# Last group's second channel product: three of seven outer products with tokens stationary, and a shared sum joined once

## The chip, the cores and the metric

The kernel runs on one core of one Trainium2 chip. The metric is the device time of one execution in microseconds (us). The time before is the median of three runs, 780.99 us (780.35 to 781.89). One more execution was taken by the hardware profiler. All times below that carry a place ("at 762.0") are us from the start of that execution's span.

TensorE (PE) multiplies matrices and writes PSUM; PEld is its weight load. VectorE (DVE), ScalarE (ACT) and GpSimd (POOL) do the rest. SyncE (SP), ScalarE and GpSimd issue DMAs.

## The reference

Inputs are q, k, v of shape (8 batches, 8 heads, 576, 64), a norm weight and four mixer weights. The part that matters here is the end:

```python
x = attention(q, k, v, g_norm)                 # (8, 576, 512)
h = np.maximum(x.T @ w_tok1, 0.0) @ w_tok2     # token mixing
u = x + h.T
h2 = np.maximum(u @ w_ch1, 0.0) @ w_ch2        # w_ch1 512 x 1536, w_ch2 1536 x 512
return u + h2
```

The change concerns the last product, `max(...) @ w_ch2`, and the addition to `u`, for the last two batches. All is float32.

## The kernel before, in words

The attention and the token mixing come first and put `u` into the output tensor in DRAM, 512 rows of each batch, and the remaining 64 rows of all batches into a ninth unit `u_rest`. Then the channel part runs over nine units of 512 rows. Unit 0 is done alone. The others go in pairs, as groups 1 to 4; the last group (g = 4) holds units 6 and 7.

In a group, both channel products are done by Strassen's scheme in Winograd's form, at two levels. The outer level has seven products (numbered 1 to 7), and each of these has seven inner products with the same numbers. The outer results of the second channel product are four quarters (i, j) of the group's output: i is the unit of the pair (unit 6 or unit 7), and j is the half of the 512 columns. With r1 to r7 for the outer results, quarter (0, 0) is r1 + r2, quarter (0, 1) is r1 + r6 + r5 + r3, quarter (1, 0) is r1 + r6 + r7 + r4, and quarter (1, 1) is r1 + r6 + r7 + r5. The sum r1 + r6 is shared by three of them. Each quarter is also added to `u`.

`outer` (line 871) writes down one outer product. It puts seven inner products at places in a list `products`, and the steps of the other engines in `beside`. Lines 1423 to 1427 then play the list place by place. So the order of all instructions on every engine is written out by hand: `put(b + place, ...)` says at which place a step is issued, where b is seven times the number of the outer product that begins the channel product. `PLACE` and `LAST` say at which place each inner product stands; the inner product 4 of an outer product stands after the first two of the next one. The last group takes its outer products in the order 1, 4, 7, 6, 5, 3, 2, the others in the order 1, 2, 4, 7, 6, 5, 3.

The PSUM banks are "a" and "b" (one each) and "d" (two). Inner product 1 fills "a"; ScalarE copies it into "d", where 6, 7 and 4 are added. Inner product 5 fills "b", and 3 is added there. Before bank "d" and bank "b" are written again, `read` saves their present state as `u2` and `p5`. Each inner result is a quarter of an outer result (128 x 256 elements) and is copied or added into it.

There are two ways to multiply (`mul`, lines 1038 to 1049). In the usual one the weights are stationary: 3 matmuls of 128 x 256 per inner product (six instructions in the profile), and the result has output columns on partitions and tokens along the free side. It lies transposed to the output, in blocks of 32. `turn` (line 1182) transposes such a tile by 32 x 32 blocks on VectorE. `put_rows` (line 1197) turns a tile and adds it to the output in DRAM by four DMAs on GpSimd that accumulate, each 128 KB in pieces of 256 B (64 columns). In the other way the tokens are stationary: 6 matmuls of 128 x 128 per inner product (twelve instructions), and the result has tokens on partitions. It lies by rows as the output does, with 256 columns in 1 KB. Before the change only outer product 2 of the last group does so (`END`).

In the last group (lines 1169 to 1174) r1 is copied to `xs`, turned and added to unit 6's left half by four accumulating DMAs. Later `fetch_last` reads that half back by rows into `xs`, product 2 is added onto it, and `store_last` writes it by four plain stores of 128 KB. Unit 6's right half is kept in a tile `xg`. It was fetched by `fetch_x` (line 599) and turned during the group before. Onto it go r1 + r6 (`xadd(6)`), r5 (`xadd(5)`) and, quarter by quarter, product 3. `store_part` (line 1202) turns it in two halves and stores it in eight pieces of 64 KB. Unit 7's two halves are joined by `join`, which is `put_rows`: r4 + r7 + r6 + r1 into the left and r7 + r6 + r1 + r5 into the right.

Of the kernel before, what the change touches and what calls it, by code (L numbers as in the profile page):

```python
# [11 lines left out]
F32 = mybir.dt.float32  # L12
# [3 lines left out]
ALU = mybir.AluOpType  # L16
# [4 lines left out]
def kernel(  # L21
# [32 lines left out]
    nc = tc.nc  # L54
    P = 128
    B, S, DM = k.shape
# [4 lines left out]
    J, JJ, HF = 4, 5, 64  # L61
    LO = P * J
    assert D == 64 and DM == 512 and S == LO + HF and B % 2 == 0
    NC, NF, NTOK = DM // P, DCH // P, DTOK // P
    HP = H // 2
    DH = DM // 2
# [5 lines left out]
    NG = 1 + B // 2  # L72
    T = 2 * P
# [4 lines left out]
    def pool(name, bufs, side="left", stack=ctx, **kw):  # L78
        return stack.enter_context(tc.tile_pool(name=name, bufs=bufs, side=side,
                                                reuse_waits="tile", **kw))  # L80
# [4 lines left out]
    left, right = ExitStack(), ExitStack()  # L85
# [24 lines left out]
    u_rows = lambda u: u_rest if u == B else out[u, :LO]  # L110

    def do(f, *a, **kw):
        return lambda: f(*a, **kw)

    late = {}


    keep = tc.keep_in_program_order

    def dma(o, i, engine=nc.sync):  # L120
        keep(engine.dma_start(o, i))

    def tensor_add(o, a, b, op=ALU.add, engine=nc.vector):
        keep(engine.tensor_tensor(out=o, in0=a, in1=b, op=op))  # L124
# [4 lines left out]
    def copy(o, a):  # L129
        keep(nc.scalar.copy(o, a))  # L130

    def matmul(*a, **kw):
        keep(nc.tensor.matmul(*a, **kw))  # L133
# [458 lines left out]
    xg, xt, uT = {}, {}, {}  # L592
    Q = 32
    NQ = T // Q

    def units(g):
        return ((0,), (1, 2), (3, 4), (5, B), (6, 7))[g] if g < NG else (NU, NU)

    def fetch_x(g):

        if g == 0:
            xg[g] = late["xg0"].tile([P, J, DM], F32, name="xg")
            dma(xg[g], u_rows(0).rearrange("(t p) e -> p t e", p=P))
        else:
            xg[g] = late["xg"].tile([P, 2 * NQ, 2, Q], F32, name="xg")
            for b in range(NC):
                dma(xg[g][ds(b * Q, Q)].rearrange("p n l j -> p n (l j)"),
                    u_rows(units(g)[0])[:, ds(DH + b * HF, HF)].rearrange("(n i) e -> i n e", i=Q))

    def fetch_t(u, i):  # L610

# [251 lines left out]
    PLACE = {1: 0, 5: 1, 6: 3, 2: 4, 3: 5, 7: 6, 4: 9}  # L863
    LAST = {1: 0, 5: 1, 6: 3, 2: 4, 7: 5, 3: 6, 4: 7}
    products, beside = {}, defaultdict(list)
    END = NG - 1, 2

    def put(place, *steps):
        beside[place] += steps
# [77 lines left out]
    def halves(f):  # L947
        return [do(f, i) for i in range(2)]
# [13 lines left out]
    def w_part(n, p):  # L962
        return ws[n, POS[p] // 2][:, POS[p] % 2]

    def fetch_ahead(n):
        for k, place in enumerate((-12, -9, -7, -4)):
            if 7 * n + place >= 0:
                put(7 * n + place, do(fetch_w, n, k))
# [61 lines left out]
    def channel2(g, n0):  # L1030
        b = 7 * n0
        t = {n: do(v_tile, g, i) for n, i in FROM.items()}

        def second(i, o):
            n = n0 + i
            r = {}

            def mul(p, ps, start, stop):
                v = v_in_parts[g, o](p)
                w = w_part(n, p).rearrange("p (w e) -> p w e", w=W)  # L1040
                if (g, o) == END:
                    for t in range(2):
                        for s in range(W):
                            matmul(ps[:, ts(t, P)], lhsT=v[:, s, ts(t, P)], rhs=w[:, s],
                                   start=(start and t == 0 and s == 0), stop=stop, skip_group_check=True)
                else:
                    for s in range(W):
                        matmul(ps, lhsT=w[:, s], rhs=v[:, s], start=(start and s == 0), stop=stop,
                               skip_group_check=True)

            def to(i, j):
                if not r:
                    name = "us" if o in (1, 2, 6, 3) else "r"
                    r[0] = late[name].tile([P, 2 * NQ, 2, Q], F32, name=name, tag=name)
                return r[0][:, ts(i, NQ), j]

            if (g, o) == END:
                outer(7 * n, T, mul, lambda i, j: rows_of(xs[0])[:, ts(i, 2), j], onto=True, last=True,
                      fit=lambda flat: flat.rearrange("p (t b e) -> p t b e", t=2, b=NC))
            elif g == NG - 1 and o == 3:  # L1060
                outer(7 * n, T, mul, lambda i, j: xg[g][:, ts(i, NQ), j], onto=True)
            else:
                outer(7 * n, T, mul, to)
            fetch_ahead(n)
            return r

        rs = {}
        for i, o in enumerate(order2(g)):
            rs[o] = second(i, o)
# [47 lines left out]
            tensor_add(half(a21(), i), half(a21(), i), half(v_tile(g, 5), i))  # L1117

        radd = lambda o, a: do(lambda: tensor_add(rs[o][0], rs[o][0], rs[a][0]))
        xadd = lambda o: do(lambda: tensor_add(*2 * [xg[g]], rs[o][0]))  # L1120
        A, S1, S2, S3, S4 = (halves(f) for f in (make_a21, sum1, sum2, sum3, sum4))


# [22 lines left out]
        def join(i, j, o):  # L1146
            return do(put_rows, units(g)[i], j, lambda: rs[o][0])

        def both(o, a, c):
# [3 lines left out]

            return step

        def first_aside():
            xs[0] = late["xs"].tile([P, 2 * NQ, 2, Q], F32, name="xs")
            copy(xs[0], rs[1][0])

        if g < NG - 1:  # L1160
            for place, *steps in ((19, radd(2, 1)), (20, join(0, 0, 2)), (38, radd(6, 1)), (39, radd(7, 6)), (40, radd(4, 7)),
                                  (41, join(1, 0, 4)), (46, radd(7, 5)), (47, radd(5, 6)), (48, join(1, 1, 7)),
                                  (52, radd(3, 5)), (55, join(0, 1, 3))):
                put(b + place, *steps)
            if g == NG - 2:
                put(b + 60, do(fetch_x, g + 1))
                put(b + 79, do(turn, lambda: xg[g + 1]))
        else:
            for place, *steps in ((11, first_aside), (17, do(put_rows, units(g)[0], 0, lambda: xs[0])), (31, radd(6, 1)),
                                  (32, radd(7, 6)), (34, fetch_last), (34, radd(4, 7)), (35, join(1, 0, 4)), (36, xadd(6)),  # L1170
                                  (38, radd(7, 5)), (39, join(1, 1, 7)), (41, xadd(5)),
                                  (44, store_part(0)), (46, store_part(1)),
                                  (48, store_last(0)), (49, store_last(1))):
                put(b + place, *steps)

# [6 lines left out]
    def turn(t):  # L1182

        t = t()
        keep(nc.vector.transpose(t, t))
# [13 lines left out]
        for b, at, to in pieces(u, j):  # L1199
            keep(nc.gpsimd.dma_start(to, t()[ds(b * Q, Q), at].rearrange("p n l j -> p n (l j)"), accum_op=ALU.add))  # L1200

    def store_part(i):

        def step():
            t = xg[NG - 1][:, ts(i, NQ)]
            turn(lambda: t)
            for b in range(NC):
                dma(out[units(NG - 1)[0], ts(i, T), ds(DH + b * HF, HF)].rearrange("(n i) e -> i n e", i=Q),
                    t[ds(b * Q, Q)].rearrange("p n l j -> p n (l j)"), nc.scalar if i and b % 2 else nc.sync)

        return step

    last_rows = lambda t=0, n=J: out[units(NG - 1)[0], ds(t * P, n * P), :DH].rearrange("(t p) e -> p t e", p=P)
    rows_of = lambda x: x.rearrange("p t (b l e) -> p t l b e", b=NC, l=2)
    xs = {}

    def fetch_last():
        xs[0] = late["xs"].tile([P, J, DH], F32, name="xs")
        dma(xs[0], last_rows())

    def store_last(i):

        def step():
            for t, queue in zip((2 * i, 2 * i + 1), (nc.sync, nc.scalar)):
                dma(last_rows(t, 1), xs[0][:, ts(t, 1)], queue)

        return step

# [126 lines left out]
    for i in range(2):  # L1355
# [4 lines left out]
    last = [  # L1360
        "h00 -i3 -d31 -s30 2 -d40 2 o0", "h01 2 o1", "h10 2 o3", "h11 2 o2", "hr z2 1 o4", "u0 z3 1 c0", "u1 z4 1 c1 o5", "u2 z5 c2",
        "u3 z6 1 c3 o6", "u4 z7 1", "u5 z8 1", "u6 1 s0", "u7 s1 s2", "u8 s3 s4"]
# [15 lines left out]
    late["c"] = pool("c", 2, "left", banks, space=bass.MemoryType.PSUM)  # L1378

    fetch_x(0)  # L1380
    firsts, lasts = mix_ch2()
    parts2 = [f for o in ORDER2 for f in split(2, o)]
# [27 lines left out]
    def turn_over():  # L1410
        w2s.close()
        late["vr"] = pool("vr", 1, "right")
        late["sv"] = pool("sv", 2, "right")
        late["s3"] = pool("s3", 1, "right")
        late["xg"] = pool("xg", 1, "right")
        late["xs"] = pool("xs", 1, "right")
        late["r"] = pool("r", 3, "right")

    put(9, turn_over)
    for g in range(1, NG):  # L1420
        channel1(g, 14 * (g - 1))
        channel2(g, 14 * (g - 1) + 7)
# [40 lines left out]
```

## Time and profile before

| what | value |
|---|---|
| median of three runs | 780.99 us (780.35 to 781.89) |
| profiled execution, its own time | 777.2 us |
| its span, first to last instruction | 775.4 us, 12776 instructions |
| granted TensorE clock | 0.999 |
| PE busy | 761.0 us, 98% |
| PEld busy | 611.6 us, 79% |
| DVE busy | 643.2 us, 83% |
| ACT busy | 277.4 us, 36% |
| POOL busy | 112.4 us, 14% |
| DMA moved | 188.30 MB, mean 243 GB/s |

The busy shares are means over the whole span. The change touches the last 30 us and two steps of some 90 us before the end. So the lines that matter are those of the end: the chain of waits from the last instruction back, the instructions in order of time, and the landings of the last DMAs. In a line of the chain stand start, length and what held it; L124 is the helper for VectorE's additions, L130 ScalarE's copy, L133 the matmul, L121 the plain DMA, L1185 the turn, and L1200 the accumulating DMA.

### The profile page before, as it was taken

How to read it: one execution, taken by the hardware profiler on the slowest of the kernel's cores; microseconds unless marked ns; L12 is line 12 of the kernel's file. 1: busy time of each engine (PE TensorE's matmuls, PEld its weight loads, DVE VectorE, ACT ScalarE, POOL GpSimd, SP SyncE). 2: the span in 40 equal slices, each digit the busy share in tenths (PEclk: the TensorE clock that was granted, in tenths of full speed). 3: DMA queues.
4: the chain of work that ended last, by engine and by line, in shares of the span. 5: the costliest groups of instructions: out<-in, count | busy, mean ns of one | idle time of the engine just before them, and what ended most of it. 6: DMA issues, size and time to landing. Idle time of an engine off the chain costs nothing.

```text
span 775.4 us, 12776 instructions
## 1 busy us (share of the span) xinstructions
PE 761.0 (98%) x4682; PEld 611.6 (79%) x4682; DVE 643.2 (83%) x946; ACT 277.4 (36%) x549; POOL 112.4 (14%) x128
## 2 busy tenths in 40 slices
PE   5999999999999999999999999999999999999997
PEld 5655555545888888888888888888888888888887
DVE  2867887897776868989978889987998996798996
ACT  2566575665210233521134242223352223325220
POOL 1002021113410000002240001042000218000204
PEclk9999999999999999999999999999999999999999
DMA  9999999999899696599998577999659879855679
GB/s 293 322 330 375 370 354 281 253 259 362 281 279 358 256 301 189 166 274 184 233 230 262 148 216 224 256 188 268 199 147 285 174 218 207 207 147 159 150 192 117
DMA packets 177820, 188.30 MB, mean 243 GB/s; under 512 B 74464, under 2 KB 140512, under 8 KB 177760
## 3 DMA queue, kind: packets, MB, share of 16 engines
q1 hardware_dynamic: 140752, 167.55, 71.5%
q0 software_dynamic: 34816, 18.36, 16.1%
q10 hardware_dynamic: 2192, 1.61, 0.7%
q8 instruction: 37, 0.61, 0.3%
q14 instruction: 23, 0.19, 0.1%
HBM read 138.31 MB, written 49.15 MB: 242 GB/s over the span
## 4 chain that ended last, share of the span: by engine, by line
PE 94%; DVE 3%; DMA 1%; ACT 1%; issue 1%; SPq 0%; DVEq 0%; ACTq 0%
PE ps_d L133 27%; PE ps_b L133 19%; PE ps_a L133 18%; PE ps_u L133 8%; PE ps_h L133 8%; PE ps_v L133 5%; PE ps_c L133 3%; PE ps_o L133 2%; PE ps_kv L133 2%; PE ps_w L133 2%; DMA raw<-in_moe_w_tok_dram 1%; ACT x L499 1%; DVE r L124 0%; DVE sv L124 0%; DVE x L445 0%
## 5 line engine op out<-in xcount | busy, mean ns | idle before, releaser
L133 PE MATMUL ps_d<-ui,w 128*128 128x256 f32 x504 | 118.6, 379 | 0.0
L133 PEld LDWEIGHTS ps_d<-ui,w 128*128 128x128 f32 x504 | 95.8, 190 | 13.0
L130 ACT COPY ps_d<-ps_a 128x768 f32<-128x768 f32 (+1 forms) x56 | 32.0, 572 | 202.1 <-PE ps_a L133 199.1
L124 DVE TENSOR_TENSOR v<-v,v 128x1536 f32<-128x1536 f32 (+2 forms) x70 | 103.2, 1482 | 0.3
L133 PE MATMUL ps_b<-sv,w 128*128 128x256 f32 x324 | 79.2, 380 | 0.1
L133 PE MATMUL ps_a<-v,w 128*128 128x256 f32 x324 | 78.8, 379 | 0.0
L1200 POOL DMA_DIRECT2D out_dram<-us x24 | 26.8, 1831 | 292.6 <-ACT p L130 287.3
L133 PEld LDWEIGHTS ps_b<-sv,w 128*128 128x128 f32 x324 | 60.8, 190 | 10.2 <-issue 2.1
L133 PEld LDWEIGHTS ps_a<-v,w 128*128 128x128 f32 x324 | 61.6, 190 | 8.4
L133 PE MATMUL ps_h<-x,w_tok 128*128 128x512 f32 (+1 forms) x160 | 65.4, 603 | 0.5 <-DVE x L503 0.4
L133 PE MATMUL ps_u<-h,w_tok 128*128 128x512 f32 (+1 forms) x160 | 64.7, 599 | 0.0
L133 PE MATMUL ps_d<-v,w 128*128 128x256 f32 x258 | 62.7, 379 | 0.0
L127 ACT ACTIVATE v<-v 128x768 f32<-128x768 f32 (+1 forms) x54 | 42.6, 821 | 55.1 <-DVE v L124 55.1
L1200 POOL DMA_DIRECT2D out_dram<-r x40 | 41.3, 1923 | 103.2 <-ACT p L130 80.3
L133 PE MATMUL ps_d<-sv,w 128*128 128x256 f32 x228 | 55.4, 379 | 0.0
L133 PEld LDWEIGHTS ps_d<-v,w 128*128 128x128 f32 x258 | 48.9, 190 | 6.6
L133 PEld LDWEIGHTS ps_h<-x,w_tok 128*128 128x128 f32 (+1 forms) x160 | 26.2, 189 | 32.3 <-issue 27.3
L133 PEld LDWEIGHTS ps_u<-h,w_tok 128*128 128x128 f32 (+1 forms) x160 | 25.6, 179 | 31.1 <-issue 26.7
L133 PEld LDWEIGHTS ps_d<-sv,w 128*128 128x128 f32 x228 | 43.3, 190 | 5.9
L133 PE MATMUL ps_a<-uT,w 128*128 128x256 f32 x192 | 46.7, 379 | 0.0
L133 PE MATMUL ps_b<-ui,w 128*128 128x256 f32 x168 | 40.8, 379 | 0.0
L133 PEld LDWEIGHTS ps_a<-uT,w 128*128 128x128 f32 x192 | 36.5, 190 | 5.0
(162 smaller groups left out, 1278.0 us busy)
## 6 DMA issues: line engine op xcount, KB each, us to landing
w<-parts SPq DMA_DIRECT2D x168, 384.0 KB, 3.7
w<-parts SPq DMA_DIRECT2D x56, 192.0 KB, 3.8
uT<-blocks SPq DMA_DIRECT2D x36, 256.0 KB, 5.3
k_in<-in_k_dram SPq DMA_DIRECT2D x16, 512.0 KB, 8.7
qT<-in_q_dram SPq DMA_DIRECT2D x8, 1024.0 KB, 9.5
out_dram<-x POOLq DMA_DIRECT2D x16, 512.0 KB, 6.4
v_in<-in_v_dram SPq DMA_DIRECT2D x14, 512.0 KB, 9.0
raw<-in_moe_w_ch_dram SPq DMA_DIRECT2D x8, 768.0 KB, 7.7
```

The costliest lines, as they stand in the source:

```text
L124: keep(engine.tensor_tensor(out=o, in0=a, in1=b, op=op))
L127: keep(nc.scalar.activation(o, a, AF.Relu))
L130: keep(nc.scalar.copy(o, a))
L133: keep(nc.tensor.matmul(*a, **kw))
L499: keep(nc.scalar.activation(x[:, k, h], x[:, k, h], AF.Copy, scale=inv[:, k, h]))
L1200: keep(nc.gpsimd.dma_start(to, t()[ds(b * Q, Q), at].rearrange("p n l j -> p n (l j)"), accum_op=ALU.add))
```

## The change

Outer products 5, 3 and 2 of the last group are now all computed with tokens stationary (`ROWS` in place of `END`). Their results lie by rows. The tile `xg` of the last group, its pool, its fetch and its early turn are gone, and so are `xadd` and `store_part`.

The shared sum r1 + r6 is joined into unit 6's right half by itself, with a turn and four accumulating DMAs. Unit 7's right half gets r7 + r6 + r1 without r5, in the same way and three places earlier. r5 is added to unit 7's right half by `join_rows`: one accumulating DMA on GpSimd of 512 rows, 1 KB each. Product 3 is written into a tile of its own. The base of its quarters is r5, so the tile holds r3 + r5. It is added to unit 6's right half by two more such DMAs of 256 rows each. Product 2 is added onto `xs` and stored as before; only the form of the tile `xs` is another.

```diff
-    END = NG - 1, 2
+    ROWS = {(NG - 1, o) for o in (5, 3, 2)}
...
-                if (g, o) == END:
+                if (g, o) in ROWS:
...
-                return r[0][:, ts(i, NQ), j]
-
-            if (g, o) == END:
-                outer(7 * n, T, mul, lambda i, j: rows_of(xs[0])[:, ts(i, 2), j], onto=True, last=True,
+                return quarter(r[0], i, j) if (g, o) in ROWS else r[0][:, ts(i, NQ), j]
+
+            if (g, o) in ROWS:
+                outer(7 * n, T, mul, (lambda i, j: quarter(xs[0], i, j)) if o == 2 else to,
+                      o == 3 and (lambda i, j: quarter(rs[5][0], i, j)), onto=o == 2, last=o == 2,
                       fit=lambda flat: flat.rearrange("p (t b e) -> p t b e", t=2, b=NC))
-            elif g == NG - 1 and o == 3:
-                outer(7 * n, T, mul, lambda i, j: xg[g][:, ts(i, NQ), j], onto=True)
...
+        def join_rows(i, o, t, n):
+            keep(nc.gpsimd.dma_start(out[units(g)[i], ds(t * P, n * P), DH:].rearrange("(t p) e -> p t e", p=P),
+                                     flat(rs[o][0])[:, ds(t, n)], accum_op=ALU.add))
...
-            if g == NG - 2:
-                put(b + 60, do(fetch_x, g + 1))
-                put(b + 79, do(turn, lambda: xg[g + 1]))
         else:
             for place, *steps in ((11, first_aside), (17, do(put_rows, units(g)[0], 0, lambda: xs[0])), (31, radd(6, 1)),
-                                  (32, radd(7, 6)), (34, fetch_last), (34, radd(4, 7)), (35, join(1, 0, 4)), (36, xadd(6)),
-                                  (38, radd(7, 5)), (39, join(1, 1, 7)), (41, xadd(5)),
-                                  (44, store_part(0)), (46, store_part(1)),
+                                  (32, radd(7, 6)), (33, join(0, 1, 6)), (34, fetch_last), (34, radd(4, 7)),
+                                  (35, join(1, 0, 4)), (36, join(1, 1, 7)), (38, do(join_rows, 1, 5, 0, J)),
+                                  (41, do(join_rows, 0, 3, 0, 2)), (45, do(join_rows, 0, 3, 2, 2)),
                                   (48, store_last(0)), (49, store_last(1))):
...
-    rows_of = lambda x: x.rearrange("p t (b l e) -> p t l b e", b=NC, l=2)
+    flat = lambda x: x.rearrange("p a b c -> p (a b c)").rearrange("p (t e) -> p t e", t=J)
+    quarter = lambda x, i, j: flat(x).rearrange("p t (b l e) -> p t l b e", b=NC, l=2)[:, ts(i, 2), j]
...
-        late["xg"] = pool("xg", 1, "right")
```

More of the change, by code (lines that the diff above doesn't have):

```diff
@@ L599, in fetch_x @@
     def fetch_x(g):
[L601 to L608, printed above, removed]
+        xg[g] = late["xg0"].tile([P, J, DM], F32, name="xg")
+        dma(xg[g], u_rows(0).rearrange("(t p) e -> p t e", p=P))
     def fetch_t(u, i):
@@ L1119, in channel2 @@
         radd = lambda o, a: do(lambda: tensor_add(rs[o][0], rs[o][0], rs[a][0]))
-        xadd = lambda o: do(lambda: tensor_add(*2 * [xg[g]], rs[o][0]))
         A, S1, S2, S3, S4 = (halves(f) for f in (make_a21, sum1, sum2, sum3, sum4))
@@ L1200, in put_rows @@
             keep(nc.gpsimd.dma_start(to, t()[ds(b * Q, Q), at].rearrange("p n l j -> p n (l j)"), accum_op=ALU.add))
[L1202 to L1211, printed above, removed]
     last_rows = lambda t=0, n=J: out[units(NG - 1)[0], ds(t * P, n * P), :DH].rearrange("(t p) e -> p t e", p=P)
-    rows_of = lambda x: x.rearrange("p t (b l e) -> p t l b e", b=NC, l=2)
+    flat = lambda x: x.rearrange("p a b c -> p (a b c)").rearrange("p (t e) -> p t e", t=J)
+    quarter = lambda x, i, j: flat(x).rearrange("p t (b l e) -> p t l b e", b=NC, l=2)[:, ts(i, 2), j]
     xs = {}
     def fetch_last():
-        xs[0] = late["xs"].tile([P, J, DH], F32, name="xs")
-        dma(xs[0], last_rows())
+        xs[0] = late["xs"].tile([P, 2 * NQ, 2, Q], F32, name="xs")
+        dma(flat(xs[0]), last_rows())
     def store_last(i):
@@ L1224, in step @@
             for t, queue in zip((2 * i, 2 * i + 1), (nc.sync, nc.scalar)):
-                dma(last_rows(t, 1), xs[0][:, ts(t, 1)], queue)
+                dma(last_rows(t, 1), flat(xs[0])[:, ts(t, 1)], queue)
         return step
```

## The prediction

> **What bounds the kernel now.** I read the page first, then the chain of waits, the instructions in order of time and the DMA issues of the last 90 us. On the page, three rows of 40 slices and the chain by engine:
>
> ```profile
> PE   5999999999999999999999999999999999999997
> DVE  2867887897776868989978889987998996798996
> POOL 1002021113410000002240001042000218000204
> ...
> PE 94%; DVE 3%; DMA 1%; ACT 1%; issue 1%; SPq 0%; DVEq 0%; ACTq 0%
> ```
>
> TensorE bounds all but the ends. VectorE follows closely. GpSimd is almost free, but it works in the last slice. The chain of waits near the end (start, length, what):
>
> ```profile
> 748.25 1.31 PE ps_b L133 x6
> 749.56 0.04 DVEq L124
> 749.60 0.55 DVE r L124 x2
> ...
> 761.63 0.32 DVE xg L124
> 761.95 0.04 issue
> 762.00 1.60 PE ps_b L133 x12
> ...
> 770.26 1.35 PE ps_d L133 x12
> 771.61 0.02 issue
> 771.63 0.42 DVE xs L124
> ```
>
> From 749.6 to 762.0 VectorE holds the chain, because it has a backlog. What TensorE loses is small: its groups start at 759.74, 762.00, and then the last at 770.10. At the pace of the other groups (6 x 1.344 + 1.296 = 9.36 us) these 10.36 us hold 1.0 us of stall. After the last sum (end 772.05) comes one store. It is issued at 772.09 and lands 2.1 us later, at 774.2. The span ends at 775.4, so 1.2 us follow the last landing. What GpSimd does, in order of time:
>
> ```profile
> 753.38 1.25 DVE L1185 STREAM_TRANSPOSE r<-r 128x1024 f32<-128x1024 f32 x1
> ...
> 755.19 4.33 POOL L1200 DMA_DIRECT2D out_dram<-r  x4 [20.23 <-ACT r L130]
> ...
> 762.19 4.36 POOL L1200 DMA_DIRECT2D out_dram<-r  x4 [2.67 <-ACT ps_d L130]
> ```
>
> The four accumulating DMAs of one join follow their turn by 0.56 us (754.63 to 755.19) and end at +1.06, then 1.09 apart. In the DMA view, cut to the stretch 765.5 to 766.0, only the last of those eight is there; it started at 764.15 and lands at 770.1:
>
> ```profile
> out_dram<-r POOLq DMA_DIRECT2D x1, 128.0 KB, 6.0
> ```
>
> That is 3.6 us after its descriptors were done at 766.55; the last of the join before (757.15 to 759.52) landed at 762.34, 2.8 us after. Between 764.2 and 764.8 nothing else moves, so that stretch gives the price of accumulating pieces of 256 B:
>
> ```profile
> DMA packets 341, 0.09 MB, mean 145 GB/s; under 512 B 341, under 2 KB 341, under 8 KB 341
> ```
>
> **What the Trainium skill says.** All on the page "DMA: Bandwidth & Descriptors". Section "SWDGE vs HWDGE vs iDMA": accumulating works only from GpSimd, which writes the descriptors itself. The trace agrees: all of line 1200 is on POOL, some 1.1 us each. Section "Anatomy of one DMA — SWDGE (gpsimd) path": about 2.0 us plus bytes by 436 GB/s; waits are held by the issuing engine before dispatch. A plain 512 KB store from GpSimd would be 3.2 us; the fastest I found in the trace took 4.2 (issue at 157.59), so the page is a floor. Section "Rules for kernel authors": an accumulate needs the landing of an earlier one on the same bytes. No run here shows such a case yet, but the change makes one. Section "Queues, rings and completion order": each DMA engine takes turns between queues. The trace fits: from 756 to 771 GpSimd's queue had 91.7% and SP's 16.3% of the engines, over 100% together.
>
> **The change part by part.** Times are of the profiled execution.
>
> *TensorE.* Products 5 and 3 of the last group have 14 inner products. Each becomes 12 short instructions (1.344 us, as product 2 has now) instead of 6 long ones (1.295): +0.05 x 14 = +0.7.
>
> *VectorE.* Gone near the end are two additions onto `xg` and `radd(7, 5)` (each 1.22, with the next starting after 1.14) and two half turns (0.70): 4.8 us. Added is one turn of product 6's sum (1.25). Product 3's six small steps (0.42) stay six, now with product 5's rows as second operand; ScalarE's copies of `p5` and `u2` of product 3 go, and VectorE reads those PSUM banks itself. I replay the new order from 749.8: join of product 5's bank, one `sv`, the turn of product 6 from 751.0 to 752.25, small step, `v`, addition to product 4, its turn to 755.7, `p5`, `sv`, turn of product 7 to 758.1, `sv`, `u2` from 758.9 to 759.3. TensorE would have got to the inner product that overwrites `u2`'s bank at 759.03 and must wait until 759.37: a new stall of 0.34. After that the backlog is gone: product 3's bank b is read at 760.8 and the next group wants it at 762.06, so the 1.0 us stall falls away.
>
> *Sum up to the last sum:* +0.7 - 1.0 + 0.34 = +0.04. The last group starts at 770.1 as before, and the last store lands near 774.2 as before. The removed loads and the early turn of `xg` lie where TensorE has no stall and VectorE later idles (1.6 us at 713.2): nothing. If their cover were gone, it would be one turn, 1.2 us, in our favour. Eight stores of 64 KB on SP and ScalarE go too; none ended last.
>
> *GpSimd.* Its DMAs near the end go from 8 to 15, in one queue, in order. Three joins stand first: product 6's sum (turned at 752.25, starts at 752.8), product 4's (ready 756.3) and product 7's (ready 758.7). Both are ready before the one ahead is through, so twelve DMAs run without a break: 752.8 + 1.06 + 11 x 1.09 = 765.85. The last lands 2.8 to 3.6 us later; I take 769.1.
> Next is the row join of product 5. It adds to the rows that product 7's join has just added to, and in the built program it waits for all four of those landings. Product 3's two row joins are ready at 762 and 765.4 but queue behind it. So this wait is the new thing. A start at 769.5 (0.4 for the release; a turn's took 0.56) and the first packet 1.6 us later (that of the DMA at 755.19 came at 756.8) give 771.1.
> Now 1 MB goes through in pieces of 1 KB, a size that the trace has in no accumulate. Low end: plain rows of 1 KB (the last stores) ran at 328 GB/s: 3.2 us. High end: no better than the 145 GB/s of 256 B pieces: 7.2 us. Between: a plain packet takes 9 ns plus 0.037 per byte (46 at 1 KB, 18 at 256 B), and the 256 B accumulates passed every 28 ns per engine, which is 9 plus twice the bytes. So 1 KB is some 84 ns, and 64 packets per engine 5.4 us. I take this, as it fits the rate seen. The last stores share the engines meanwhile (512 KB, 1.5 us of their time; I take 1.0), and 0.5 passes from last packet to landing. Landing: 771.1 + 5.4 + 1.0 + 0.5 = 778.0. With 1.2 to the end: 779.2, or +3.8. As turns shared between queues may overlap, I take +3.5. The median of the runs shown, 780.99, is above the profiled execution (777.2, span 775.4) for reasons that the change doesn't touch, so I add: **784.5 us**.
> Ends: 3.2 us of transfer and no sharing give +0.6, or 781.6. Landing of the joins at 768.7 takes that to 781.2. 7.2 us and 1.5 of sharing give +6.1, and a late release 787.5.
>
> **The rivals.**
> *The row joins are hidden.* If the joins land by 768.5 and rows of 1 KB accumulate as fast as plain ones, the last landing (768.5 + 0.4 + 1.6 + 3.2 + 0.5) is at 774.2 and ties with the last store: 780.5 to 782.5, not slower. For it: large pieces should use the engines better, and the plain store of 512 KB took only 4.2. Against: 1 MB and three DMAs queue behind a start of about 769.5, just 4.7 us before the landing that now ends it. It decides when all of product 3's rows land by 775.8 (+1.56).
> *Accumulating costs as much per byte at 1 KB, or GpSimd's descriptors run out of room.* Each packet took 46 ns at 256 B; four times that and no overlap are 184 ns, 11.8 us: 791. More than eight joins in a row are not in the trace. For it: bursts stop near 600 packets per us; against: that is 9 ns plus twice the bytes.
> *VectorE becomes the bound.* `p5` and `u2` now wait in its line. If it is 1 us later, TensorE ends near 772.6, which the row joins hide. Alone it gives 782.
> *It saves what it removes.* Had GpSimd no tail, the best is the stall of 1.0 less 0.7: 780.7. No gain over 0.2% (1.56 us, about what a measurement of this kernel can tell from no change) can come of it.
>
> **How the numbers follow.** Row joins end last at a price between the ends: 0.64 (own range 782.6 to 787.5, likeliest 784.5). The dear accumulate: 0.13 (787 to 791). Hidden or tied, VectorE's bound among them: 0.20 (780.0 to 782.5). A gain that I don't see: 0.03. The range leaves one in ten on either side: 781.3 to 788.3. Faster 0.03, same (to 782.55) 0.20, slower 0.77.
>
> **What would show it.** Twelve accumulates on POOL from 752.8 without a break; the row joins starting around 769.5; landings of rows after 775; the chain ending in a DMA and not in `xs`. TensorE's 0.7 us gap at 762 gone, and one of 0.3 before product 3's seventh inner product. I am wrong if the row joins start before 767 (then the landing wait is cheaper than I think), if they take under 4 us in all, or if TensorE ends over 1 us from 771.6.

## The result and the profile after

The kernel after takes 784.95 us (784.4 to 788.46), the kernel before, with the runs taken beside it, 779.62 us (778.43 to 781.89): a ratio of 1.0075, 95% interval 1.005 to 1.010, which is 5.8 us slower (3.9 to 7.8). By the medians alone it is 5.3 us. The profiled execution of after took 787.1 us, its span 785.3, at a mean clock of 0.997. The clock does not explain the loss: from 190 us to the last sum it was 1.00 in both, and after's mean is lowered by the end, where TensorE has nothing left to do (0.75 from 776 to 785).

Two profiled executions of the same program can differ by some us long before the change: at 147 us TensorE of after waits 2.85 us for `qT<-in_q_dram`, where before it waited 0.59 us at 143.8, and the change touches neither. At the first matmuls of the channel part (`ps_v`) after is already 3.82 us behind, in the chain of before and then of after (start, length, what):

```profile
188.78 36.46 PE ps_v L133 x168
192.60 36.46 PE ps_v L133 x168
```

From there to the start of VectorE's last sum (`xs<-ps_d`) it is 582.85 us in before and 583.02 in after (583.00 to 583.04 in all other runs whose last sum is in the trace, but for one). So nearly all of the difference ahead of that sum arose before the channel part, and the change itself added 0.17. I therefore compare ends by the *tail*, the time from the start of that sum to the end of the span. Before it is 775.43 - 771.63 = 3.8 us, after 785.35 - 775.62 = 9.7 us: +5.9. A second profiled execution of after (the run "after_again" below, whose last sum starts at 773.04) has +6.0.

The page of after, with two rows of its 40 slices and the chain by engine:

```profile
PE   6899999899999999999999999999999999999995
DVE  2757887797776868989979889996989996898991
...
PE 90%; DMA 7%; POOL 1%; issue 1%; POOLq 0%; ACTq 0%; ACT 0%; SPq 0%
```

In the last slice TensorE falls from 7 tenths to 5 and VectorE from 6 to 1: they are through, and the span goes on. In the chain DMA has risen from 1% to 7%, but most of that is not the end: loads of the first 147 us make up some 43 us of it, and the end only the 7.92 us below, 1% of the span. Such a share has to be read together with its place. The chain of waits from 754 us on (start, length, what):

```profile
764.56 7.92 DMA out_dram<-r
...
773.91 1.77 POOL out_dram L1149
775.68 1.24 POOLq L1440
```

No TensorE and no VectorE is left here. The chain is a landing (7.92 us, to 772.48), then the row joins (L1149, here the first of product 3), and then GpSimd at the kernel's last line (L1440), where it signs off once all has landed. The chain as printed breaks off at 776.92; what is left to 785.3 is landings and that sign-off. In order of time (start, busy, engine, line, what, and in brackets the idle time before it with what ended that):

```profile
756.67 4.33 POOL L1193 DMA_DIRECT2D out_dram<-us  x4 [17.91 <-issue]
759.99 9.75 POOL L1193 DMA_DIRECT2D out_dram<-r  x8
...
763.25 1.60 PE L133 MATMUL ps_d<-w,v 128*128 128x128 f32 x12 [0.30 <-DVE u L124]
...
773.13 1.32 POOL L1149 DMA_DIRECT2D out_dram<-r  x1 [3.39 <-DMA out_dram<-r]
773.91 3.01 POOL L1149 DMA_DIRECT2D out_dram<-us  x2
...
774.73 1.93 SPq L121 DMA_DIRECT2D out_dram<-xs  x2
775.62 0.42 DVE L124 TENSOR_TENSOR xs<-ps_d,xs 128x256 f32<-128x256 f32 x1 [0.92 <-PE ps_d L133]
```

The twelve DMAs of the three joins run without a break (756.67 to 769.74). Then GpSimd is idle for 3.39 us until the last of them has landed, and only then issues the row join of product 5, with product 3's two right behind it. They were issued 2.5 to 1.0 us before the last sum. When they and the last stores land is in the DMA view from 690 us on (name, queue, count, KB each, median us from issue to landing):

```profile
out_dram<-r POOLq DMA_DIRECT2D x1, 512.0 KB, 6.2
out_dram<-us POOLq DMA_DIRECT2D x2, 256.0 KB, 8.4
out_dram<-xs SPq DMA_DIRECT2D x2, 128.0 KB, 5.3
```

The same view of before, for SyncE's two last stores:

```profile
out_dram<-xs SPq DMA_DIRECT2D x2, 128.0 KB, 1.8
```

Product 5's rows land at 779.34, product 3's at 782.00 and 783.25. The last stores, which nothing in the program ties to the row joins, land at 779.77 to 781.89: 5.0 to 5.8 us after their issue. What the engines moved from 774 to 784 us, in slices of 0.25 us:

```profile
GB/s 0 0 0 0 98 102 53 82 156 201 197 201 197 201 197 197 197 303 365 348 238 217 233 254 270 266 254 275 222 201 193 197 201 176 33 4 0 0 0 0
```

The first row packets come at 775.0, slowly for a microsecond (53 to 102 GB/s). From 776.25 to 778.25 product 5's rows run at 197 GB/s. The peak of 303 to 365 at 778.25 to 779.0 is mostly not rows: it is the first pair of last stores (one by SyncE and one by ScalarE), whose first packet went at 778.16, 3.4 us after its issue. From 779.25 on, product 3's rows and the second pair share the engines, and from 781.25 the rest of the rows runs alone at about 197.

### The profile page after: what moved, and what is told of

It is laid out like the page before. It is cut to its first block, busy times and chain, and to the rows that moved or that the text cites. A ratio compares the mean times of both kernels' runs of the same rounds, so it can differ in the third digit from the quotient of the medians.

```text
span 785.3 us, 12927 instructions
## 1 busy us (share of the span) xinstructions
PE 762.8 (97%) x4766; PEld 615.7 (78%) x4766; DVE 638.7 (81%) x941; ACT 276.6 (35%) x547; POOL 120.4 (15%) x135
## 4 chain that ended last, share of the span: by engine, by line
PE 90%; DMA 7%; POOL 1%; issue 1%; POOLq 0%; ACTq 0%; ACT 0%; SPq 0%
PE ps_d L133 26%; PE ps_a L133 18%; PE ps_b L133 18%; PE ps_u L133 8%; PE ps_h L133 7%; PE ps_v L133 5%; PE ps_c L133 3%; DMA v_in<-in_v_dram 2%; PE ps_w L133 2%; PE ps_kv L133 2%; PE ps_o L133 2%; DMA qR<-in_q_dram 1%; DMA out_dram<-r 1%; DMA k_in<-in_k_dram 1%; POOL out_dram L1193 1%; DMA qT<-in_q_dram 1%
## 5 line engine op out<-in xcount | busy, mean ns | idle before, releaser
L1193 POOL DMA_DIRECT2D out_dram<-us x28 | 31.1, 1818 | 310.5 <-ACT p L130 287.3
L133 PE MATMUL ps_b<-sv,w 128*128 128x256 f32 x300 | 73.4, 380 | 0.1
L133 PE MATMUL ps_a<-v,w 128*128 128x256 f32 x300 | 72.9, 379 | 0.0
L133 PEld LDWEIGHTS ps_b<-sv,w 128*128 128x128 f32 x300 | 56.3, 190 | 9.6 <-issue 2.1
L133 PEld LDWEIGHTS ps_a<-v,w 128*128 128x128 f32 x300 | 57.0, 190 | 7.8
L133 PE MATMUL ps_d<-v,w 128*128 128x256 f32 x234 | 56.9, 379 | 0.0
L133 PE MATMUL ps_d<-sv,w 128*128 128x256 f32 x216 | 52.5, 379 | 0.0
L133 PEld LDWEIGHTS ps_d<-v,w 128*128 128x128 f32 x234 | 44.4, 190 | 6.0
L133 PEld LDWEIGHTS ps_d<-sv,w 128*128 128x128 f32 x216 | 41.0, 190 | 5.6
L121 POOL DMA_DIRECT2D out_dram<-x x24 | 16.3, 681 | 159.6 <-DVE x L124 129.3
```

## Experiments

The theories: A, that the row joins end last because of their place: behind twelve joins and their landing; against it, that the price of the accumulating transfers decides (B in the expectations); and C, that TensorE or VectorE has become later before the last sum. Two more came later: R, that product 3 is better added to rows read back and stored plainly, and that the last stores are held up by the rows. The table collects what was measured. Ratios are to runs of before on the same chip. "Row issues" and the landings are us from the start of the last sum, from each profile; in each row the row joins stand in the order of issue.

| run | ratio [95%] | row issues | row joins land | last stores land | tail against before |
|---|---|---|---|---|---|
| after | 1.0075 [1.0050, 1.0100] | -2.5, -1.7, -1.0 | 3.7, 6.4, 7.6 | 4.2 to 6.3 | +5.9 |
| after_again | 1.0095 [1.0072, 1.0118] | -2.4, -1.7, -0.9 | 3.8, 6.4, 7.7 | 4.2 to 7.2 | +6.0 |
| e1_rows5_first | 1.0042 [1.0022, 1.0062] | -16.0, -4.4, -3.6 | -7.5, 2.3, 5.0 | 2.6 to 5.0 | +3.7 |
| e2_rows3_first | 1.0047 [1.0030, 1.0064] | -10.3, -6.0, -2.6 | -1.7, 0.5, 5.3 | 4.0 to 6.1 | +3.6 |
| e3_no_row_joins | 1.0004 [0.9986, 1.0022] | none | none | 1.0 to 2.6 | +0.1 |
| e4_plain_rows | 1.0028 [1.0016, 1.0041] | -2.3, -1.5, -0.8 | 1.5, 2.8, 4.0 | 3.7 to 4.4 | +2.3 |
| e7_rows5_elsewhere | 1.0065 [1.0040, 1.0089] | -10.4, -8.0, -6.0 | 1.1, 2.5, 4.2 | 4.5 to 5.3 | +3.2 |
| e8_between | 1.0003 [0.9989, 1.0018] | -16.0, -10.6, -5.4 | -8.6, -2.8, 2.6 | 3.0 to 4.1 | +2.0 |
| e9_rows3_stored | 1.0051 [1.0038, 1.0064] | -16.4 | -8.1 | 3.2 to 4.1 | +1.8 |
| e10_no_rows5 | 0.9998 [0.9981, 1.0015] | -9.9, -6.0 | -1.0, 0.4 | 1.1 to 2.5 | +0.4 |
| e11_no_rows3 | 1.0030 [1.0014, 1.0046] | -2.4 | 3.3 | 3.8 to 4.7 | +2.6 |

(Before: last stores land up to 2.6.) All edits are to the kernel after.

### Product 5's rows ahead of the joins of 4 and 7

Products 4 and 7 are turned in place at their old places on VectorE, and only their accumulating DMAs move behind the row join of product 5 (the last argument `True` leaves out the turn in `put_rows`).

```diff
-(35, join(1, 0, 4)), (36, join(1, 1, 7)), (38, do(join_rows, 1, 5, 0, J)),
+(35, do(turn, lambda: rs[4][0])), (36, do(turn, lambda: rs[7][0])), (38, do(join_rows, 1, 5, 0, J)),
+(38, do(put_rows, units(g)[1], 0, lambda: rs[4][0], True)), (38, do(put_rows, units(g)[1], 1, lambda: rs[7][0], True)),
```

> The changed kernel with one thing moved: on GpSimd the row join of product 5 goes ahead of the DMAs of products 4's and 7's joins (their turns on VectorE stay where they are), so that nothing at the end waits for a landing. Theory A (the wait for product 7's landings, with all rows queued behind it, sets the end): the last landing is again that of product 2's store, and the time is that of the kernel before within 1.5 us, some 5 to 6 us under the changed kernel. Theory B (1 MB of row accumulates costs its engine time wherever it stands): at least 2.5 us over the kernel before. Theory C (TensorE and VectorE lost the time): unchanged, over 4.5 us over the kernel before.

It took 781.6 us, 1.0042: better than after, but not level. Theory A's 1.5 us is missed, and theory B's range (at least 2.5) is met. The order of time in its profile:

```profile
756.37 2.70 POOL L1149 DMA_DIRECT2D out_dram<-r  x1
...
765.39 4.33 POOL L1195 DMA_DIRECT2D out_dram<-r  x4 [1.91 <-DVE xs L124]
```

The row join no longer waits, but product 7's join now does. It adds to the same bytes, and begins at 765.39, 0.6 us after product 5's rows have landed (764.81); the bracket names VectorE, which was long done. Product 3's rows stand behind that join and land 5.0 us after the last sum. The wait was turned round, not taken away, so this run does not part A from B.

### Product 5's rows last

```diff
-(35, join(1, 0, 4)), (36, join(1, 1, 7)), (38, do(join_rows, 1, 5, 0, J)),
-(41, do(join_rows, 0, 3, 0, 2)), (45, do(join_rows, 0, 3, 2, 2)),
+(35, join(1, 0, 4)), (36, join(1, 1, 7)),
+(41, do(join_rows, 0, 3, 0, 2)), (45, do(join_rows, 0, 3, 2, 2)), (45, do(join_rows, 1, 5, 0, J)),
```

> The changed kernel with product 5's row join put behind product 3's two on GpSimd, so that only product 5's rows still wait for product 7's landings and half the bytes are through before. Theory A (wait plus what is queued behind it): +1.7 us over the kernel before (+0.5 to +3). Theory B (the sum of the row bytes decides): as the changed kernel, +4.5 or more. Theory C: as the changed kernel.

It took 781.75 us, 1.0047, with a tail of +3.6 where at most +3 was expected. In its DMA view from 760 us on:

```profile
out_dram<-r POOLq DMA_DIRECT2D x1, 512.0 KB, 7.9
out_dram<-xs SPq DMA_DIRECT2D x2, 128.0 KB, 5.2
```

Product 3's rows are out of the way 0.5 us after the last sum. But product 5's start no sooner than in after (-2.6 against -2.5), still behind the landing of product 7's join, and take 7.9 us. The last stores take 5.2 us and land last of all, at +6.1. I had counted the rows alone and not what they do to the stores.

### Without the row joins

All three row joins are left out, so unit 7 lacks r5 and unit 6 lacks r3 + r5; the rest is as in after.

```diff
-(35, join(1, 0, 4)), (36, join(1, 1, 7)), (38, do(join_rows, 1, 5, 0, J)),
-(41, do(join_rows, 0, 3, 0, 2)), (45, do(join_rows, 0, 3, 2, 2)),
+(35, join(1, 0, 4)), (36, join(1, 1, 7)),
```

> The changed kernel without the three row joins: products 5 and 3 are computed and summed but not added to the output, so its right halves of units 6 and 7 lack them. Theories A and B: the end is product 2's store again, the time is that of the kernel before within 1.5 us. Theory C (TensorE's 14 slower inner products and VectorE's order made it slower): it stays 4 us or more over the kernel before.

It took 778.69 us, 1.0004 [0.9986, 1.0022], with a tail of +0.1. In its DMA view from 760 us on:

```profile
out_dram<-xs SPq DMA_DIRECT2D x2, 128.0 KB, 1.9
```

The last stores take what they took before. The longer inner products, the changed order on VectorE and the third join are all still in this kernel, and together cost nothing that the times can tell (from `ps_v` to the last sum 583.01 us, 0.16 over before). So C falls, and the whole loss hangs on the row joins. It says a second thing: with that work gone altogether the kernel is level with before. So no placing of the row joins can be expected to win more than the interval of this run allows, some 1 us.

### Plain rows in place of accumulating ones

The three row DMAs write instead of adding, so those two halves hold r5 and r3 + r5 alone.

```diff
-flat(rs[o][0])[:, ds(t, n)], accum_op=ALU.add))
+flat(rs[o][0])[:, ds(t, n)]))
```

> The changed kernel with the three row DMAs as plain stores in place of accumulates, in the same order and with the same waits; the output's right halves then hold the rows alone. If the doubled price of an accumulated byte is part of it (64 packets per DMA engine at 46 in place of 84 ns), it is 2.4 us under the changed kernel, +3.4 over the one before (+2 to +4.3). If the wait alone decides: no less than +5.

It took 780.3 us, 1.0028, with a tail of +2.3, in the range. In its DMA view from 760 us on:

```profile
out_dram<-r POOLq DMA_DIRECT2D x1, 512.0 KB, 3.8
out_dram<-us POOLq DMA_DIRECT2D x2, 256.0 KB, 4.5
```

Wait and start are as in after (-2.3). The rows land at +4.0 in place of +7.6. So the accumulating price is 3.6 us of the tail of 5.9, and 2.3 us would remain with plain rows at the same place. The edit changes a second thing: these plain rows went in packets of 4 KB, the accumulating ones in packets of 1 KB. The 3.6 us are for both together.

### After without the last stores

`store_last` is left out, so unit 6's left half lacks product 2.

```diff
-(41, do(join_rows, 0, 3, 0, 2)), (45, do(join_rows, 0, 3, 2, 2)),
-(48, store_last(0)), (49, store_last(1))):
+(41, do(join_rows, 0, 3, 0, 2)), (45, do(join_rows, 0, 3, 2, 2)),):
```

> The changed kernel without the four plain stores of product 2 at the end, so the output's last left half stays without product 2. The row joins are as in the changed kernel. Theory S (the last stores and the row accumulates slow each other on the shared DMA engines): the rows land some 2 us sooner after their start, 10.1 us becoming 8, and the time is +3.5 us over the kernel before (+2.5 to +4.5). Theory N (sharing costs nothing; the rows alone take that long): no change against the changed kernel, +5 or more.

It took 783.26 us, 1.0057 [1.0035, 1.0079]: 4.4 us over before, in the range. In its DMA view from 760 us on:

```profile
out_dram<-r POOLq DMA_DIRECT2D x1, 512.0 KB, 6.5
out_dram<-us POOLq DMA_DIRECT2D x2, 256.0 KB, 7.3
```

From the first row issue (770.52) to the last landing (779.65) are 9.1 us, in after 10.1 (773.13 to 783.25). So the stores cost the rows 1.0 us, and not the 2 that the expectation put (8 us were expected here). What is above my estimate is in the rows' own transfer. VectorE's last sum is missing from this trace. The three sums before it start 1.34 to 1.35 us apart, so I put it at 772.92; the tail is then +5.0, an estimate.

### Product 5's rows to other bytes

They are added to unit 0's right half, so that no landing has to be waited for. Unit 0 has r5 too many and unit 7 lacks it.

```diff
-keep(nc.gpsimd.dma_start(out[units(g)[i], ds(t * P, n * P), DH:].rearrange("(t p) e -> p t e", p=P),
+u = 0 if o == 5 else units(g)[i]
+keep(nc.gpsimd.dma_start(out[u, ds(t * P, n * P), DH:].rearrange("(t p) e -> p t e", p=P),
```

> The changed kernel with product 5's rows added to unit 0's right half in place of unit 7's: the same bytes and the same order on GpSimd, but no earlier DMA touches those rows at that time, so nothing is waited for (the output is another in both places). Theory A (the wait for the landings): the rows start right behind product 7's join, 3.3 us sooner, and meet the last stores less: +1.2 us over the kernel before (+0.3 to +2.5). Theory Q (GpSimd's queue of fifteen DMAs and the row bytes decide, the wait is covered by them): +4 or more.

It took 784.04 us, 1.0065 [1.0040, 1.0089], which the times do not tell from after, and which lies in theory Q's range (+4 or more). The tail was +3.2, not the +1.2 expected. In its DMA view from 760 us on:

```profile
out_dram<-r POOLq DMA_DIRECT2D x1, 512.0 KB, 11.6
...
out_dram<-xs SPq DMA_DIRECT2D x2, 128.0 KB, 5.0
```

The idle stretch of GpSimd is gone, and the rows land 2.6 to 3.9 us sooner (+1.1, +2.5, +4.2). But they still run under the last stores, and those now land last, at +5.3. By this trace the wait is a real part (2.8 us of the tail), and not all of it. The times of the six executions do not confirm the 2.8; why they lie above what the tail says stays open.

### Product 3's rows between the joins

Product 5's rows go ahead of the join of product 4, product 3's first rows ahead of the join of product 7; all the work is done.

```diff
-(35, join(1, 0, 4)), (36, join(1, 1, 7)), (38, do(join_rows, 1, 5, 0, J)),
-(41, do(join_rows, 0, 3, 0, 2)), (45, do(join_rows, 0, 3, 2, 2)),
+(35, do(turn, lambda: rs[4][0])), (36, do(turn, lambda: rs[7][0])), (38, do(join_rows, 1, 5, 0, J)),
+(38, do(put_rows, units(g)[1], 0, lambda: rs[4][0], True)), (41, do(join_rows, 0, 3, 0, 2)),
+(41, do(put_rows, units(g)[1], 1, lambda: rs[7][0], True)), (45, do(join_rows, 0, 3, 2, 2)),
```

> All of the work, in another order on GpSimd: product 6's join, product 5's rows, product 4's join, product 3's first rows, product 7's join, product 3's last rows. Product 7's join is then the one that waits for product 5's rows, but these have had product 4's join and the first rows of product 3 as cover; only 256 KB of rows come after. If wait and collision at the end are all there is to it: within 1.5 us of the kernel before (+0.5). If GpSimd's signing off after its last landing and its 15 DMAs keep a cost: +2 to +3, as with product 5's rows alone moved.

It took 779.9 us, 1.0003 [0.9989, 1.0018]: the best of all that do the whole work, and not to be told from before. The order of time in its profile:

```profile
767.24 2.97 POOL L1149 DMA_DIRECT2D out_dram<-us  x1
769.53 5.06 POOL L1195 DMA_DIRECT2D out_dram<-r  x4
```

Product 3's first rows (line 1149) fill the time in which product 7's join (line 1195) waits for product 5's rows. The last rows land at +2.6, and only the last stores still suffer (+4.1). Its profiled execution took 785.4 us, 5.5 above its median. It was behind before the channel part began: it came to `ps_v` at 194.80, 6.0 us later than before, with a granted clock of 0.96 from 100 to 190 us where before had 1.00. Its tail is +2.0. The times hold a part of that: the median is 1.1 us over the 778.79 of the runs of before beside it, and the fastest execution 1.2 us over their fastest. So this order takes away most of the loss; a rest of about a microsecond is neither shown nor excluded.

### Product 3 added to rows read back

In the order of the first experiment, product 3 is added on VectorE to the right half of unit 6, read back by rows, and stored by one plain DMA from SyncE. All the work is done.

```diff
-(41, do(join_rows, 0, 3, 0, 2)), (45, do(join_rows, 0, 3, 2, 2)),
...
+(38, do(put_rows, units(g)[1], 1, lambda: rs[7][0], True)), (39, fetch_right), (44, do(store_right, rs)),
...
+def fetch_right():
+    xs[1] = late["xq"].tile([P, 2 * NQ, 2, Q], F32, name="xq")
+    dma(flat(xs[1]), right_rows)
...
+def store_right(rs):
+    tensor_add(xs[1], xs[1], rs[3][0])
+    dma(right_rows, flat(xs[1]))
...
```

> All of the work, with products 5, 3 and 2 by rows, but product 3's rows don't accumulate: unit 6's right half is read back by rows after product 6's join, the tile of product 3 is added to it on VectorE (one addition, 1.14 us, in an idle stretch), and one plain store on SP writes it some 5 us before TensorE ends. On GpSimd product 5's rows come second, and nothing comes after product 7's join. Theory R (what accumulates beside and after the last stores made the time): the tail past TensorE's end is +0.3 us over that of the kernel before (0 to +1), the time within 1.5 us of it. Theory G (rows as such, or more than eight accumulating DMAs in a row, cost time): +2 or more.

It took 782.63 us, 1.0051 [1.0038, 1.0064]. R is missed, and theory G's range (+2 or more) is met. The order of time in its profile:

```profile
767.52 0.38 SPq L121 DMA_DIRECT2D xq<-out_dram  x1
...
775.37 1.23 DVE L124 TENSOR_TENSOR xq<-xq,us 128x1024 f32<-128x1024 f32 x1 [2.73 <-DMA xq<-out_dram]
```

The read-back landed 7.75 us after its issue (775.27): it moved beside the accumulates. VectorE, whose list is in order, stood 2.73 us before the addition, and product 2's sums behind it came late. The tail (+1.8) does not hold that delay, which lies ahead of the last sum. But most of it was made up again: from `ps_v` to the last sum it is 583.41 us, only 0.6 over before. Tail and delay are 2.4 us together, the time is 4.0 over before; where the rest comes from stays open.

### After once more

No edit.

> The changed kernel itself, beside the run above on the same chip: tail past TensorE's end +5.9 us over that of the kernel before, as in its first profile, within 0.5; the time +5 to +6.5.

785.2 us, 1.0095 [1.0072, 1.0118]. The tail of +6.0 is as expected; the time, +6.8 us by the medians, lies a little above the +5 to +6.5. The last sum of this execution starts 2.6 us earlier than in the first, and the tail is the same within 0.04 us.

### Each product's rows alone

First without product 5's rows (unit 7 lacks r5):

```diff
-(35, join(1, 0, 4)), (36, join(1, 1, 7)), (38, do(join_rows, 1, 5, 0, J)),
+(35, join(1, 0, 4)), (36, join(1, 1, 7)),
```

> The changed kernel without product 5's row join (unit 7's right half then lacks product 5); product 3's two row joins stay where they are. They follow product 7's join on GpSimd and have nothing to wait for. If they cost only because they stand behind product 5's wait: their landing some 1 us past TensorE's end, the tail +0.5 us over the kernel before (0 to +1), the time within 1.5 us. If 512 KB of rows near the end cost by themselves: tail +2 or more.

Then without product 3's (unit 6 lacks r3 + r5):

```diff
-(41, do(join_rows, 0, 3, 0, 2)), (45, do(join_rows, 0, 3, 2, 2)),
```

> The changed kernel without product 3's two row joins (unit 6's right half then lacks products 3 and 5); product 5's stays, with its wait for product 7's landings. Its 512 KB start 2.4 us before TensorE's end and share the engines with the last stores: landing some 3.8 us past TensorE's end, 1.4 us of signing off by GpSimd and 0.7 to the end: tail +2.1 over the kernel before (+1.5 to +3). If the wait alone made all of the loss: +5 or more.

Both came out as expected: 778.07 us (0.9998, tail +0.4) and 781.33 us (1.0030, tail +2.6). The DMA view from 760 us on, first of the one with product 3's rows alone:

```profile
out_dram<-us POOLq DMA_DIRECT2D x2, 256.0 KB, 7.6
out_dram<-xs SPq DMA_DIRECT2D x2, 128.0 KB, 1.9
```

And of the one with product 5's rows alone:

```profile
out_dram<-r POOLq DMA_DIRECT2D x1, 512.0 KB, 5.7
out_dram<-xs SPq DMA_DIRECT2D x2, 128.0 KB, 4.4
```

Product 3's rows, issued behind the joins with nothing to wait for, are hidden (landing at +0.4), and the stores run free. Product 5's rows alone land at +3.3 and push the stores to +4.7: those end the kernel. Alone the two cost 0.4 and 2.6, together 5.9. The missing 2.9 us come when product 3's rows stand in line behind product 5's wait and transfer: with them they are issued at -1.7 and -1.0, without at -9.9 and -6.0.

## Why the prediction was right in sign and time, and short in size

The predicted time of 784.5 us lies 0.45 from the measured median, partly by luck: the step from the base of 780.99 was +3.5, and measured are +5.3 by the medians (+5.8 by the ratio) on a base of 779.62. So two errors of opposite sign nearly cancelled. The mechanism is shown: the row joins, behind twelve joins and a landing, end last. Two terms of the sum were too small, and the last stores were missing as a second ending. The sum gave +3.8; the 0.3 taken off for overlap between queues have no support in the runs. To set the profile of after beside the predicted places I take off 3.99 us, the difference of the two last sums (775.62 - 771.63).

- **Up to the last sum: +0.04 forecast, +0.17 measured** (583.02 for 582.85 us from `ps_v` on). The stall of 0.34 before product 3's seventh inner product is there (0.30 at 763.25), the 0.7 us gap at 762 is gone, and without the row joins the kernel is level (1.0004).
- **Twelve DMAs without a break: confirmed.** Start 752.7 for 752.8, end 765.75 for 765.85.
- **The wait for the landing: confirmed.** 3.39 us on GpSimd. The last join landed at 768.5, 2.7 us after its descriptors, just under the 2.8 to 3.6 that I had, so 0.6 sooner than the 769.1 taken; the row join began at 769.1 for 769.5, and the first packet went at 771.0 for 771.1.
- **The rate of 1 KB accumulates: confirmed.** 197 GB/s are 12.3 per engine, and so 83 ns for 1 KB; 84 were forecast. So 9 ns plus twice 0.037 ns per byte, which fitted the 28 ns of 256 B, fits at 1 KB too, and the dear accumulate (184 ns) fell.
- **The transfer, 5.4 + 1.0: 1.5 us short.** From the first to the last row packet it took 7.9 us (775.0 to 782.93). The sharing was right: 1.0, by the run without the last stores, which still needs 6.9 for the rows alone. What I left out are the stretches in which the rows run below 197 GB/s. In that run they are the start (102 GB/s over the first 0.6 us), 1.5 us around the change from product 5 to product 3 (156 GB/s), and the last 1.4 us (75 GB/s). In after the start is slow as well (84 GB/s from 775 to 776). The half microsecond from 778.5, in which hardly a row moved, belongs to the sharing: the last stores filled it, at 357 GB/s in all. I had priced 1 MB as one stream.
- **The end, 1.2: 0.9 us short.** From the last landing (783.25) to the end are 2.1 us. I took the 1.2 from before, where the last landing in the trace is a store of ScalarE's. GpSimd's sign-off begins no sooner than 1.36 us after the last landing of its own (1.36 to 1.37 in after, its repeat, and the runs with product 5's rows ahead of the joins or last, with plain rows and without the last stores). In before GpSimd's own had long landed (770.12); the last landing was at 774.23, and the sign-off began 0.5 us later.
- Sum: 3.8 + 1.5 + 0.9, less 0.1 for the start and 0.2 from packet to landing (0.3 for 0.5), is 5.9, the tail measured.
- **The last stores: seen as sharers, and that only.** I counted what they take from the rows. That the rows hold them to 5.0 to 5.8 us, so that they would end the kernel by themselves (+2.6 with product 5's rows alone), was in no step. Where the rows are moved forward it shows: in three of the variants (product 5's rows last, product 5's rows to other bytes, and product 3's rows between the joins) the last stores land last of all, at +6.1, +5.3 and +4.1.

Of the rivals, "the row joins are hidden" asked that all of product 3's rows land by 775.8. On before's clock they landed at 779.26, so it fell. VectorE did not become the bound. "It saves what it removes" was put at 0.3 us at best, and nothing was seen. One reading of the prediction does not hold: that two queues with over 100% of the engines together show the turns between queues. From 764.2 to 764.8 in before GpSimd's queue alone stands at 168.7%, so packets of one queue overlap already.

What the Trainium skill states in "DMA: Bandwidth & Descriptors", section "Rules for kernel authors", that an accumulate has to wait for an earlier DMA on the same bytes, is now in the traces as a wait: 3.39 us here, and 1.91 in the first experiment with the two turned round. With product 5's rows sent to other bytes there was none. What happens without the wait no run here shows.

## What to carry to other kernels

Before moving a sum out of VectorE into an accumulating DMA near the end, write down the line of GpSimd's queue with its landings: in these programs an accumulate onto bytes that another has just touched starts only after that one's landing, and all behind it in the queue wait along. Let the DMA that has nothing to wait for fill that wait, as in the version that came nearest to before. And price what such a stream does to the stores that end the kernel, not only what they do to it.

## What the runs showed of the hardware

- A plain store issued 0.3 us before the first packets of product 5's row join moved nothing for 3.4 us (issue 774.73, first packet 778.16), until product 5's rows were nearly through; with product 5's rows alone it was much the same (771.89, first packet 775.22). It is not the addition alone: with plain rows it moved nothing from 771.50 to 773.31. In before its first packet came within 1.0 us of the issue. Beside product 3's rows the second pair did share the engines (249 GB/s in all from 779.25 to 781.25). The Trainium skill, "DMA: Bandwidth & Descriptors", section "Queues, rings and completion order", says that an engine drains a whole packet of descriptors from one ring before it switches. That would fit, if product 5's 32 rows per engine were one such packet. No run here varied that number, and product 3's 16 rows per engine and DMA did not hold the stores up, so the cause stays open.
- The descriptors of a row join took GpSimd 1.32 us for 512 rows and about as long for 256 (1.24), by the chain and the order of time: the number of rows hardly counted. As plain stores they took 0.81 and some 0.7.
- The first dozen packets of product 5's row join took about 250 ns each (medians of 243 to 268 in after, its repeat, and the runs without product 3's rows and without the last stores), later ones 102, passing every 83 ns per engine.
